# Moving all loads but the first queries to SyncE's queue, with three transfers in place of six for the global values, and the order of the work drawn up anew

## The chip, the cores and the metric

The kernel runs on one core of a Trainium2 chip. The metric is device microseconds of one execution; a profile of one execution comes with it. The engines are named as in the profile: PE is TensorE, DVE is VectorE, ACT is ScalarE, POOL is GpSimd, SP is SyncE. SP does no arithmetic here; it only issues DMA transfers, and so can ACT and POOL. "PEld" is the loading of weights into TensorE, "q1" the queue on which SP issues, "q0" that of POOL, "q10" that of ACT. Lines such as L323 are lines of the kernel before; the diff shifts them by a few in the changed kernel.

## The reference

Attention with a window of 32 positions and 32 global tokens for 8 batches, 8 heads, 512 positions and head size 64; after it an MLP over all 4,352 rows of the result, 512 wide, with 2,048 inner units. In the attention's result and in the MLP all is float32, except that the two weight matrices are float64.

```python
k_all, v_all = concat([k_g, k_l], 2), concat([v_g, v_l], 2)
out_g = softmax(scale * q_g @ k_all.T) @ v_all          # 32 global queries see all 544 keys
s_ll  = where(|i - j| <= 32, scale * q_l @ k_l.T, -1e9) # local queries see a band ...
s_l   = concat([scale * q_l @ k_g.T, s_ll], -1)         # ... and the 32 global keys
out_l = softmax(s_l) @ v_all
x     = concat([out_g, out_l], 2) as (8 * 544, 512)
h     = x @ w_in                                        # 512 -> 2048
out   = (0.5 * h * (1 + erf(h / sqrt(2)))) @ w_out      # 2048 -> 512
```

## The kernel before

**Tiles.** A *unit* is (batch, half, pair): 256 queries of two heads. There are 8 x 2 x 4 = 64 units. Four units give 256 rows of the MLP's input; so the MLP has 16 *pieces* of 256 rows, and a 17th ("g") for the 8 x 32 global queries. A piece goes through the inner units in 16 steps of 128: `h` (L915 to L917, twelve matmuls of 128x256), Gelu, and `mo` (L947 to L949, six matmuls of 128x512 that add into two accumulators). Most products are taken as three: each float32 operand is split into a part rounded to float32r and the rest, and high x high, low x high and high x low are added. The splits are copies (L293 on ACT, L295 on DVE) and subtractions (L303 on POOL or DVE).

**Weights.** `w_load` (L323, L327) brings, for each of the 16 steps, a pair of 512 KB transfers of float64 bits: one of `w_in` (n even) and one of `w_out` (n odd), 32 transfers in all. Steps `w1` to `w5` make float32 of them and split it: L334 and L338 on ACT, L342 on DVE, the rounded copy on DVE or ACT, and the rest on DVE (L303). There are five buffers `wpair`; the sixth pair waits until `w5` of the first is done. After that all weights stay in SBUF. So the first MLP piece can go no faster than the weights are loaded and converted.

**Attention.** For the first 8 units (`NPE`), keys and queries arrive in natural order and are transposed on TensorE (`st_tkn` L516 to L518, `st_tqn` L524). They come in three groups, units 0 and 1, 2 and 3, and 4 to 7; their loads are few and large: `load_kn` (L498, L501), `load_qn` (L508), `load_v` (L443 to L454). The transposes write to PSUM; copies to `kq` (L293 or L295) free that buffer again. For all later units, `load_k` (L409) and `load_q` (L414) bring blocks of 32 columns, four transfers each, which DVE transposes (L480, L481, L529). Then follow the scores (`st_s` L607), the masked minimum (L626 on DVE), the exponential (L471 on ACT), the normalisation, transposes of the weights (`st_t` L678) and the products with the values (L714, L727). The first 8 units (`NF32`) do scores and products in plain float32, all later ones in split form.

**Global values.** For each pair of heads `gu_load` (L831, L833) fills the tile `gvr`, the first 640 columns of `raws`: two transfers bring the 512 local values of each head, and four bring the *same* 32 global values to all four blocks of 32 partitions of the last 128 columns. The matrix they are multiplied with has zeros in three of the blocks, so three of the four copies only keep the operand finite.

**What sets the order.** The order is fixed when the kernel is built, by a planner at its end. Every piece of work is a `step` with an engine (or several to choose from), a duration (`DUR`), needs, buffers that it takes and frees, and a due time. The due time is a formula plus offsets: `OFF`, `OFF0` (one for each kind of step), `UO` (each of the first 16 units), `WO` (each weight transfer) and `XO` (single steps). The planner simulates all engines and the DMA queues and takes, engine by engine, the startable step with the earliest due time; the resulting sequence is written into each engine's program. Engines work through their programs strictly in that order: an instruction that waits holds up all that stands behind it on its engine, and a transfer that waits for a buffer holds up all later transfers of its queue. In the planner's account of the DMA, a queue that has eight transfers in flight takes no further one until the oldest has landed.

Queues in the kernel before: keys, values and global loads on SP (`LKE`, `LVE`, and `nc.sync` written out in `load_k`, `load_q`, `load_g`, `gu_load`); the queries of units 0 to 3 on ACT, those of units 4 to 7 on SP (`LQE`); weight transfers 0 to 15 on POOL (`PQ = 16`), the others on POOL or SP as the planner chooses (`WLE = "ps"`). In effect 21 weight transfers were issued by POOL and 11 by SP.

Of the kernel before, what the change touches and what calls it, by code (L numbers as in the profile page):

```python
# [42 lines left out]
AHEAD = 7.79  # L43
# [7 lines left out]
    "ah": -28.3, "al": 190.6, "c": 36.0, "e": -46.4, "g": -91.8, "gagh": 105.3, "gagl": 84.4, "gah": 95.0,  # L51
    "gal": 279.0, "gex": 364.9, "gh": 34.3, "gl": 79.7, "glv": -266.7, "gmin": 286.5, "gn": -288.8,
    "go": -250.4, "gsh": -53.2, "gsl": -34.5, "gt": -14.4, "gvc": -55.9, "gvl": -83.0, "gx": -45.8,
# [6 lines left out]
}  # L60
OFF0 = {
# [7 lines left out]
PW = 6.14  # L69
PA = 14.0  # L70
UO = [-160.8, -144.7, -220.4, -102.2, -9.8, 29.6, 12.6, -140.0, 234.7, -181.3, -185.0, -209.3, -93.2, -116.0, -6.6, -119.4]
WO = [-219.9, -117.6, -1.3, -67.8, -468.9, -339.8, -131.7, -537.2, 29.9, 77.1, 219.1, 469.3, 117.1, 46.4, -152.0, -101.1, -73.4, 224.9, 158.3, 77.0, 133.5, -203.0, -360.4, 13.9, 12.3, 251.1, 181.3, 156.0, 275.5, 162.0, 44.8, 157.5]
FA = 86.16
PU = 5.1
NF32 = 8
WLE = "ps"
PQ = 16
XO = {
# [17 lines left out]
    ('g', (0, 1), 4): 14.9, ('gagh', (0, 0)): 46.1, ('gagh', (0, 1)): 21.0, ('gagl', (0, 0)): -65.7,  # L96
    ('gagl', (0, 1)): 66.1, ('gah', (0, 0), 0): -6.3, ('gah', (0, 0), 1): 5.8, ('gah', (0, 1), 0): -22.2,
    ('gah', (0, 1), 1): -21.7, ('gal', (0, 0), 0): 15.1, ('gal', (0, 0), 1): 3.3, ('gal', (0, 1), 0): -36.9,
    ('gal', (0, 1), 1): 52.6, ('gex', (0, 0)): 185.8, ('gex', (0, 1)): -30.8, ('gh', (0, 0), 0): -8.2,
# [6 lines left out]
    ('glv', (0, 0), 1): 19.3, ('glv', (0, 1), 0): 49.6, ('glv', (0, 1), 1): -159.6, ('glv', (1, 0), 0): 10.1,  # L106
    ('glv', (1, 0), 1): 0.5, ('gmin', (0, 0)): 135.0, ('gmin', (0, 1)): 4.0, ('gn', (0, 0)): -64.2,
    ('gn', (0, 1)): -43.6, ('go', (0, 0), 0): 117.3, ('go', (0, 0), 1): 87.3, ('go', (0, 1), 0): -62.5,
    ('go', (0, 1), 1): -69.7, ('gsh', (0, 0), 0): 53.1, ('gsh', (0, 0), 1): 24.9, ('gsh', (0, 1), 0): 5.6,
    ('gsh', (0, 1), 1): 16.4, ('gsl', (0, 0), 0): 35.1, ('gsl', (0, 0), 1): 4.3, ('gsl', (0, 1), 0): 40.5,  # L110
    ('gsl', (0, 1), 1): -47.7, ('gt', (0, 0)): 66.4, ('gt', (0, 1)): 17.2, ('gvc', (0, 0), 0): -44.9,
    ('gvc', (0, 0), 1): -265.4, ('gvc', (0, 1), 0): 35.8, ('gvc', (0, 1), 1): -57.0, ('gvl', (0, 0), 0): -51.9,
    ('gvl', (0, 0), 1): -114.2, ('gvl', (0, 1), 0): 51.6, ('gvl', (0, 1), 1): -111.7, ('gvl', (1, 0), 0): -35.8,
    ('gx', (0, 0), 0): 17.2, ('gx', (0, 0), 1): 2.6, ('gx', (0, 1), 0): -23.5, ('gx', (0, 1), 1): -1.5,
    ('gyh', (0, 0), 0): -7.7, ('gyh', (0, 0), 1): 85.4, ('gyh', (0, 1), 0): 167.6, ('gyl', (0, 0), 0): -50.7,
# [1279 lines left out]
```

## Time and profile before

| | |
|---|---|
| median of 3 runs | 1057.9 us (1053.37 to 1058.07) |
| the profiled execution | 1057.46 us, its span 1055.7 us |
| PE busy | 1016.4 us (96%) |
| PEld busy | 903.3 us (86%) |
| ACT busy | 758.4 us (72%) |
| DVE busy | 681.8 us (65%) |
| POOL busy | 352.8 us (33%) |
| mean granted TensorE clock | 0.987 |
| bytes moved by DMA | 71.25 MB, mean 67 GB/s |

Busy shares are means over the whole span. The span has an opening, in which weights and the first units are loaded, a long even stretch, and an end; these are to be read apart, with the view of busy time by stretch. In the lists of waits a row names the waiting instruction, what it waited for, the total in us, the number of waits and the longest. In the chain of waits, each row is a piece of the chain that ended last: start, length, and what it was.

### The profile page before, as it was taken

The page shows a single profiled execution, that of the slowest core. Times are in us where ns is not written, and L with a number is a line of the kernel's source. Part 1 is how long each engine was busy: PE and PEld are TensorE (multiplying, and loading weights), DVE is VectorE, ACT ScalarE, POOL GpSimd, SP SyncE. Part 2 cuts the span into 40 slices and gives each one's busy share as a digit, 9 for nine tenths or more (in the row PEclk, how much of TensorE's full clock was granted, in tenths as well). Part 3 has the DMA queues.
Part 4 walks back from the last instruction along what each step waited for, and adds up shares of the span by engine and source line. Part 5 has one row for each costly group of instructions (what it writes and reads, how often), then busy time and mean ns, then how long its engine had stood idle before and what let it go on. Part 6 is the DMA issues. An engine that isn't in the chain of part 4 may idle for free.

```text
span 1055.7 us, 21420 instructions
## 1 busy us (share of the span) xinstructions
PE 1016.4 (96%) x7100; PEld 903.3 (86%) x7100; DVE 681.8 (65%) x2052; ACT 758.4 (72%) x1628; POOL 352.8 (33%) x410
## 2 busy tenths in 40 slices
PE   5687999999999999999999999999999999999998
PEld 2365898989889898899889898999889898998897
DVE  2887866866775866877677766877677766751000
ACT  3797777977777888677777887787877887763221
POOL 4222233334232532334322523334223423343121
PEclk9698999999999999999999999999999999999999
DMA  9746232223322232223312331323322331110000
GB/s 286 178 149 210 66 80 60 44 64 61 70 38 50 58 83 39 61 45 67 69 33 56 60 85 35 67 40 70 68 36 53 67 78 35 47 26 21 1 21 21
DMA packets 268255, 71.25 MB, mean 67 GB/s; under 512 B 257776, under 2 KB 260336, under 8 KB 268144
## 3 DMA queue, kind: packets, MB, share of 16 engines
q1 hardware_dynamic: 262912, 58.21, 25.4%
q0 software_dynamic: 3024, 11.01, 3.0%
q8 instruction: 56, 0.92, 0.4%
q10 hardware_dynamic: 2208, 0.66, 0.3%
q14 instruction: 55, 0.45, 0.2%
HBM read 60.88 MB, written 8.91 MB: 66 GB/s over the span
## 4 chain that ended last, share of the span: by engine, by line
PE 89%; DMA 4%; DVE 3%; ACT 2%; issue 1%; SPq 1%; ACTq 0%; DVEq 0%
PE h L915 12%; PE h L917 12%; PE h L916 11%; PE acc L947 11%; PE acc L948 11%; PE acc L949 11%; PE o L714 5%; PE s L607 5%; PE t L678 2%; PE go L848 2%; PE sg L758 1%; PE t L679 1%; DMA kn<-in_k_l_dram 1%; DMA wpair<-in_moe_w_out_dram 1%; DMA vr<-in_v_g_dram 1%
## 5 line engine op out<-in xcount | busy, mean ns | idle before, releaser
L915 PE MATMUL h<-xx,w 128*128 128x256 f32 x1088 | 314.5, 289 | 4.0 <-ACT gf L471 4.0
L303 POOL TENSOR_TENSOR gl<-gf,gh 128x512 fp32r<-128x512 f32 x135 | 176.2, 1306 | 400.8 <-ACT gh L293 225.8
L917 PE MATMUL h<-xx,w 128*128 128x256 f32 x1088 | 304.6, 280 | 4.4 <-DVE w L303 4.4
L916 PE MATMUL h<-xx,w 128*128 128x256 f32 x1088 | 304.0, 279 | 0.0
L947 PE MATMUL acc<-w,gh 128*128 128x512 f32 x544 | 221.1, 406 | 0.0
L915 PEld LDWEIGHTS h<-xx,w 128*128 128x128 f32 x1088 | 204.9, 188 | 15.6 <-ACT gf L471 4.6
L948 PE MATMUL acc<-w,gl 128*128 128x512 f32 x544 | 215.1, 395 | 0.0
L949 PE MATMUL acc<-w,gh 128*128 128x512 f32 x544 | 215.0, 395 | 0.0
L916 PEld LDWEIGHTS h<-xx,w 128*128 128x128 f32 x1088 | 205.1, 188 | 6.4
L917 PEld LDWEIGHTS h<-xx,w 128*128 128x128 f32 x1088 | 204.8, 188 | 5.3 <-DVE w L303 5.3
L471 ACT ACT_TABLE_LOAD x141 | 180.9, 1283 | 5.6 <-PE h L917 3.1
L303 POOL TENSOR_TENSOR vs<-vr,vs 128x512 fp32r<-128x512 f32 x56 | 74.6, 1332 | 191.0 <-ACT vs L293 87.3
L471 ACT ACTIVATE gf<-h 128x512 f32<-128x512 f32 x136 | 81.5, 599 | 70.0 <-PE h L917 35.0
L949 PEld LDWEIGHTS acc<-w,gh 128*128 128x128 f32 x544 | 102.5, 188 | 24.5
L471 ACT ACTIVATE a_t<-a_t,sm 128x192 f32<-128x192 f32 x240 | 109.8, 459 | 14.0 <-DVE sm L626 13.2
L947 PEld LDWEIGHTS acc<-w,gh 128*128 128x128 f32 x544 | 102.5, 188 | 14.0 <-issue 0.3
L948 PEld LDWEIGHTS acc<-w,gl 128*128 128x128 f32 x544 | 102.8, 189 | 12.9
L626 DVE CUSTOM_DVE_ANT_0 a_t<-s,mask 128x192 f32<-128x192 f32 x240 | 76.2, 368 | 29.7 <-PE s L607 29.0
L293 ACT ACTIVATE gh<-gf 128x512 fp32r<-128x512 f32 x88 | 55.6, 632 | 49.0 <-PE acc L949 47.8
L698 DVE TENSOR_TENSOR at<-t,at 128x512 fp32r<-128x512 f32 (+1 forms) x112 | 68.1, 616 | 28.9 <-ACT at L293 27.6
L714 PE MATMUL o<-at,vs 128*128 128x256 f32 x448 | 74.2, 288 | 0.3
L293 ACT ACTIVATE at<-t 128x512 fp32r<-128x512 f32 (+1 forms) x112 | 59.1, 541 | 18.6 <-PE t L679 12.0
(138 smaller groups left out, 1573.7 us busy)
## 6 DMA issues: line engine op xcount, KB each, us to landing
raws<-in_v_l_dram SPq DMA_DIRECT2D x64, 128.0 KB, 2.5
out_dram<-ob SPq DMA_DIRECT2D x32, 256.0 KB, 2.3
raws<-in_k_l_dram SPq DMA_DIRECT2D x224, 36.0 KB, 2.0
vr<-in_v_l_dram SPq DMA_DIRECT2D x112, 64.0 KB, 2.1
raws<-in_q_l_dram SPq DMA_DIRECT2D x224, 32.0 KB, 1.9
wpair<-in_moe_w_in_dram POOLq DMA_DIRECT2D x11, 512.0 KB, 8.1
wpair<-in_moe_w_out_dram POOLq DMA_DIRECT2D x10, 512.0 KB, 8.6
wpair<-in_moe_w_out_dram SPq DMA_DIRECT2D x6, 512.0 KB, 5.4
```

Source lines behind the costliest of these rows:

```text
L293: nc.scalar.activation(out=out, in_=in_, func=AF.Copy)
L303: (nc.vector if e == "v" else nc.gpsimd).tensor_sub(**kw)
L471: nc.scalar.activation(func=func, **kw)
L626: nc.vector.tensor_tensor_reduce(out=a_t[:, j, aoff[half][i]:aoff[half][i] + w], in0=s[:, c:c + w], in1=masks[half][:, c:c + w], scale=-SC ...
L698: nc.vector.tensor_sub(out=at[:, 1], in0=st.pop((u, "t", j))[:, :n * P].rearrange("p (n q) -> p n q", q=P), in1=at.bitcast(F32)[:, 0])
L714: nc.tensor.matmul(out=o[:, :, qsl], lhsT=l.rearrange("p s e -> p (s e)"), rhs=r, start=(n == 0), stop=(n == 3), skip_group_check=True)
L915: nc.tensor.matmul(out=h, lhsT=hi, rhs=xh, start=(c == 0), stop=False, skip_group_check=True)
L916: nc.tensor.matmul(out=h, lhsT=hi, rhs=xl, start=False, stop=False, skip_group_check=True)
L917: nc.tensor.matmul(out=h, lhsT=lo, rhs=xh, start=False, stop=(c == NCC - 1), skip_group_check=True)
L947: nc.tensor.matmul(out=acc[t], lhsT=gh[:, f % 2, tsl], rhs=hi, start=(f == a), stop=False)
L948: nc.tensor.matmul(out=acc[t], lhsT=gl[:, f % 2, tsl], rhs=hi, start=False, stop=False)
L949: nc.tensor.matmul(out=acc[t], lhsT=gh[:, f % 2, tsl], rhs=lo, start=False, stop=(f == b - 1))
```

## The change

All weight transfers are issued by SP (`WLE = "s"`, `PQ = 0`), and the queries of units 2 and 3 too; only the two query transfers of units 0 and 1 stay on ACT. `load_k`, `load_q`, `load_g` and `gu_load` take their queue from the planner (`queue(e)`), which is given SP alone for them. `gu_load` issues one transfer of the global values in place of four; the three blocks of partitions that it no longer writes are zeroed once by a memset at the start. The planner's durations of the plain float32 scores are set to 1.2 and 0.65 (1.05 and 0.55 before), its constants and all offsets are new, and so the order of the steps on every engine is another one.

```diff
-    "o": 0.48, "s0": 1.05, "sg0": 0.55, ...
+    "o": 0.48, "s0": 1.2, "sg0": 0.65, ...
...
-AHEAD = 7.79
+AHEAD = 21.61
...
-PW = 6.14
+PW = 7.45
...
-FA = 86.16
-PU = 5.1
+FA = 122.95
+PU = 9.25
...
-WLE = "ps"
-PQ = 16
+WLE = "s"
+PQ = 0
...
-LQE = {0: "a", 2: "a", 4: "s", 6: "s"}
+LQE = {0: "a", 2: "s", 4: "s", 6: "s"}
...
     raws = cp.tile([P, 1184], F32, name="raws")
+    nc.gpsimd.memset(raws[:, 512:640], 0.0)
...
 def load_k(e, u):
-            nc.sync.dma_start(out=kraw[pr], ...)
+            queue(e).dma_start(out=kraw[pr], ...)
...
 def gu_load(e, g, i):
         for j in range(2):
-            nc.sync.dma_start(out=raw[:, j:8:2, :], in_=v_l[b, 2 * p + j].rearrange("(t s) e -> s t e", s=P))
-        for n in range(4):
-            nc.sync.dma_start(out=raw[32 * n:32 * n + 32, 8:10, :], in_=v_g[b, 2 * p:2 * p + 2].rearrange("h s e -> s h e"))
+            queue(e).dma_start(out=raw[:, j:8:2, :], in_=v_l[b, 2 * p + j].rearrange("(t s) e -> s t e", s=P))
+        queue(e).dma_start(out=raw[0:32, 8:10, :], in_=v_g[b, 2 * p:2 * p + 2].rearrange("h s e -> s h e"))
...
-                step(("glv", g, i), gu_load, (g, i), "s", g0 - 12.0 + 2 * i, [], [("gvr", (g, i))], issues=6, size=0.46, ...)
+                step(("glv", g, i), gu_load, (g, i), "s", g0 - 12.0 + 2 * i, [], [("gvr", (g, i))], issues=3, size=0.42, ...)
```

The tables `OFF`, `OFF0`, `UO`, `WO` and `XO` are left out: every number in them is replaced, and `XO` has more entries.

More of the change, by code (lines that the diff above doesn't have):

```diff
@@ L50 @@
 OFF = {
-    "ah": -28.3, "al": 190.6, "c": 36.0, "e": -46.4, "g": -91.8, "gagh": 105.3, "gagl": 84.4, "gah": 95.0,
-    "gal": 279.0, "gex": 364.9, "gh": 34.3, "gl": 79.7, "glv": -266.7, "gmin": 286.5, "gn": -288.8,
-    "go": -250.4, "gsh": -53.2, "gsl": -34.5, "gt": -14.4, "gvc": -55.9, "gvl": -83.0, "gx": -45.8,
[6 rows of a table removed]
+    "ah": -211.1, "al": 160.1, "c": -16.3, "e": 13.1, "g": -47.0, "gagh": 62.8, "gagl": 136.9,
+    "gah": 55.5, "gal": 309.1, "gex": 12.5, "gh": -21.6, "gl": 127.7, "glv": -432.6, "gmin": 325.2,
+    "gn": -164.9, "go": -134.3, "gsh": 61.6, "gsl": -288.7, "gt": 23.5, "gvc": -30.4, "gvl": 21.8,
[6 rows of a table added]
 }
 OFF0 = {
[4 rows of a table removed]
[4 rows of a table added]
 }
@@ L68 @@
 FH = 8
-PW = 6.14
+PW = 7.45
 PA = 14.0
-UO = [-160.8, -144.7, -220.4, -102.2, -9.8, 29.6, 12.6, -140.0, 234.7, -181.3, -185.0, -209.3, -93.2, -116.0, -6.6, -119.4]
-WO = [-219.9, -117.6, -1.3, -67.8, -468.9, -339.8, -131.7, -537.2, 29.9, 77.1, 219.1, 469.3, 117.1, 46.4, -152.0, -101.1, -73.4, 224.9, 158.3, 77.0, 133.5, -203.0, -360.4, 13.9, 12.3, 251.1, 181.3, 156.0, 275.5, 162.0, 44.8, 157.5]
-FA = 86.16
-PU = 5.1
+UO = [-392.3, -324.5, -466.6, -352.7, -219.4, -4.3, 79.2, -212.3, 297.9, -231.0, -224.0, -213.8, -190.2, -142.1, -206.7, -54.7]
@@ L75 @@
+WO = [-233.6, -272.1, 18.8, 79.4, -468.3, -440.1, 10.1, -401.7, 160.7, 127.2, 284.8, 552.5, 98.0, 88.9, -36.8, -133.1, -19.5, 157.0, 203.3, 10.3, 3.9, -137.0, -448.4, 17.1, -86.0, 50.4, 66.1, -73.3, 84.2, -14.7, -33.4, 3.9]
+FA = 122.95
+PU = 9.25
 NF32 = 8
-WLE = "ps"
-PQ = 16
+WLE = "s"
+PQ = 0
 XO = {
[17 rows of a table removed]
[L96 to L99, printed above, removed]
[6 rows of a table removed]
[L106 to L115, printed above, removed]
[54 rows of a table removed]
-    ('sga', (0, 0, 2)): 14.5, ('sga', (0, 0, 3)): -31.2, ('sga', (0, 1, 0)): 74.4, ('sga', (0, 1, 1)): 6.0,
-    ('sga', (0, 1, 2)): 18.2, ('sga', (0, 1, 3)): 3.3, ('sga', (1, 0, 0)): -162.1, ('sga', (1, 0, 1)): -106.7,
-    ('sga', (1, 0, 2)): -11.1, ('sgc', (1, 0, 0)): -7.9, ('sgc', (1, 0, 1)): 68.0, ('sgc', (1, 0, 2)): -81.1,
[42 rows of a table removed]
[19 rows of a table added]
+    ('gagl', (0, 0)): -47.6, ('gagl', (0, 1)): 17.8, ('gah', (0, 0), 0): 36.0, ('gah', (0, 0), 1): 34.5,
+    ('gah', (0, 1), 0): -22.0, ('gah', (0, 1), 1): 38.1, ('gal', (0, 0), 0): -245.5, ('gal', (0, 0), 1): 91.2,
+    ('gal', (0, 1), 0): 137.9, ('gal', (0, 1), 1): 13.8, ('gex', (0, 0)): 53.2, ('gex', (0, 1)): -193.4,
[7 rows of a table added]
+    ('glv', (0, 1), 0): 62.5, ('glv', (0, 1), 1): -201.2, ('glv', (1, 0), 0): -62.3, ('glv', (1, 0), 1): -12.2,
+    ('gmin', (0, 0)): 276.7, ('gmin', (0, 1)): -18.9, ('gn', (0, 0)): -31.4, ('gn', (0, 1)): 12.5,
+    ('go', (0, 0), 0): 1.7, ('go', (0, 0), 1): 229.8, ('go', (0, 1), 0): -314.7, ('go', (0, 1), 1): -76.3,
+    ('gsh', (0, 0), 0): -60.2, ('gsh', (0, 0), 1): -125.5, ('gsh', (0, 1), 0): -74.6, ('gsh', (0, 1), 1): 15.3,
+    ('gsl', (0, 0), 0): 39.4, ('gsl', (0, 0), 1): 83.0, ('gsl', (0, 1), 0): 28.1, ('gsl', (0, 1), 1): -71.6,
+    ('gt', (0, 0)): 79.7, ('gt', (0, 1)): -124.9, ('gvc', (0, 0), 0): -116.3, ('gvc', (0, 0), 1): -243.4,
+    ('gvc', (0, 1), 0): -55.5, ('gvc', (0, 1), 1): 56.6, ('gvc', (1, 0), 0): 66.2, ('gvl', (0, 0), 0): -40.7,
+    ('gvl', (0, 0), 1): -73.6, ('gvl', (0, 1), 0): -2.3, ('gvl', (0, 1), 1): -173.1, ('gvl', (1, 0), 0): 139.3,
+    ('gx', (0, 0), 0): -103.3, ('gx', (0, 0), 1): 81.1, ('gx', (0, 1), 0): -105.6, ('gx', (0, 1), 1): 50.1,
+    ('gyh', (0, 0), 0): -41.4, ('gyh', (0, 0), 1): 27.2, ('gyh', (0, 1), 0): 248.2, ('gyh', (0, 1), 1): -30.0,
+    ('gyl', (0, 0), 0): -233.3, ('gyl', (0, 0), 1): 138.1, ('gyl', (0, 1), 0): 36.2, ('gyl', (0, 1), 1): 43.6,
[57 rows of a table added]
+    ('sga', (0, 0, 1)): -68.9, ('sga', (0, 0, 2)): 214.8, ('sga', (0, 0, 3)): -2.0, ('sga', (0, 1, 0)): 202.1,
+    ('sga', (0, 1, 1)): 67.5, ('sga', (0, 1, 2)): 18.5, ('sga', (0, 1, 3)): 35.9, ('sga', (1, 0, 0)): -165.4,
+    ('sga', (1, 0, 1)): 112.4, ('sga', (1, 0, 2)): -156.5, ('sga', (1, 0, 3)): 44.0, ('sgc', (1, 0, 0)): 55.3,
+    ('sgc', (1, 0, 1)): 141.6, ('sgc', (1, 0, 2)): -79.3, ('sgc', (1, 0, 3)): 49.7, ('t', (0, 0, 0), 0): -299.1,
[42 rows of a table added]
@@ L408, in load_k @@
         for j, pr, es in quads():
-            nc.sync.dma_start(out=kraw[pr], in_=k_l[b, 2 * p + j].rearrange("(c r) e -> r c e", r=32)[:, k0:k0 + 9, es])
+            queue(e).dma_start(out=kraw[pr], in_=k_l[b, 2 * p + j].rearrange("(c r) e -> r c e", r=32)[:, k0:k0 + 9, es])
     def load_q(e, u):
@@ L413, in load_q @@
         for j, pr, es in quads():
-            nc.sync.dma_start(out=qraw[pr], in_=q_l[b, 2 * p + j].rearrange("(c r) e -> r c e", r=32)[:, 8 * half:8 * half + 8, es])
+            queue(e).dma_start(out=qraw[pr], in_=q_l[b, 2 * p + j].rearrange("(c r) e -> r c e", r=32)[:, 8 * half:8 * half + 8, es])
     gq = raws[0:SG, 0:2 * NP * D]
@@ L428, in load_g @@
             for j, pr, es in quads():
-                nc.sync.dma_start(out=dst[pr], in_=src[b].rearrange("(p j) r e -> j r p e", j=2)[j][:, :, es])
+                queue(e).dma_start(out=dst[pr], in_=src[b].rearrange("(p j) r e -> j r p e", j=2)[j][:, :, es])
     def load_v(e, u, n=1):
@@ L1141, in attn_mlp @@
                 step(("gal", g, i), gu_al, (g, i), "v", g0 + 3.0 + 2 * i, [("gah", g, i)], [], [("s", (g, "t"))])
-                step(("glv", g, i), gu_load, (g, i), "s", g0 - 12.0 + 2 * i, [], [("gvr", (g, i))], issues=6, size=0.46, after=("glv", *pi) if pi[0] else None)
+                step(("glv", g, i), gu_load, (g, i), "s", g0 - 12.0 + 2 * i, [], [("gvr", (g, i))], issues=3, size=0.42, after=("glv", *pi) if pi[0] else None)
                 step(("gvc", g, i), gu_vc, (g, i), "va", g0 + 1.0 + 2 * i, [("glv", g, i), ("late",)], [("vgs", (g, i))])
```

266 rows, old and new, of tables (DUR, OFF, OFF0, XO) are left out of this document.

## The prediction

> **What bounds the kernel now.** The time of the profiled execution is 1057.46 us, its span 1055.7 us; the 1.8 us around the span are carried along unchanged. The median of the three runs is 1057.9 us, so a sum against the profiled execution stands 0.4 us under the median. I first cut the span into three stretches with the view of busy time by stretch (columns: stretch, its length, busy time and count of PE, PEld, DVE, ACT, POOL, then granted clock, DMA share, GB/s).
>
> ```profile
> span 1055.7 us, 21420 instructions
> ...
> 0.00:140.00 140.00, 106.64 (x696) 81.84 (x697) 97.89 (x229) 103.00 (x206) 45.37 (x79) 0.90 0.60 172
> 140.00:1045.00 905.00, 903.85 (x6381) 817.01 (x6381) 583.26 (x1822) 652.98 (x1420) 307.45 (x331) 1.00 0.25 52
> 1045.00:1055.70 10.70, 5.91 (x27) 4.47 (x25) 0.69 (x1) 2.43 (x4) 0.00 (x0) 0.99 0.18 49
> ```
>
> From 140 to 1045 us TensorE is idle for 905.00 - 903.85 = 1.15 us at full clock. No new order can gain anything worth naming there; it could only lose. The last 10.7 us are the end of the last MLP and its stores, which keep their form. What can move lies in the first 140 us, where TensorE is idle for 140 - 106.64 = 33.4 us. The same view in steps of 10 us shows where:
>
> ```profile
> 0.00:10.00 10.00, 4.47 (x18) 2.81 (x20) 0.75 (x1) 3.22 (x7) 9.28 (x29) 1.00 0.88 215
> 10.00:20.00 10.00, 3.23 (x12) 1.28 (x9) 1.27 (x8) 3.96 (x11) 2.99 (x11) 1.00 1.06 359
> ...
> 30.00:40.00 10.00, 3.58 (x15) 2.12 (x15) 9.76 (x14) 9.33 (x13) 2.04 (x4) 0.57 0.84 210
> 40.00:50.00 10.00, 9.00 (x44) 5.23 (x43) 7.00 (x24) 6.67 (x21) 2.35 (x4) 0.57 0.60 120
> ...
> 90.00:100.00 10.00, 6.73 (x47) 5.39 (x45) 4.03 (x8) 5.47 (x6) 0.02 (x1) 0.99 0.93 306
> 100.00:110.00 10.00, 5.40 (x18) 4.63 (x19) 9.93 (x16) 9.20 (x16) 2.91 (x2) 0.50 0.66 217
> ```
>
> Three holes: at 10 to 20 us (6.8 us idle), at 30 to 40 us (6.4 us idle), at 90 to 110 us (3.3 + 4.6 = 7.9 us idle). The second and third are followed by a granted clock of 0.57 and 0.50, and that costs again: 0.43 x (3.58 + 9.00) = 5.4 us and 0.50 x 5.40 = 2.7 us of what counts as busy. So the holes weigh 6.8, 11.8 and 10.6 us, together 29.2 us. The first 10 us (5.5 us idle) are mostly the time until the first loads land. Next I asked for TensorE's waits in these stretches (total, times, longest), and for the pieces of the chain of waits there (start, length, what):
>
> ```profile
> PE kp L516 <- DMA kn<-in_k_l_dram: 4.4, 1, 4.4
> PE kp L518 <- DMA kn<-in_k_l_dram: 2.4, 1, 2.4
> ...
> PE kp L516 <- ACT kq L293: 8.2, 1, 8.2
> ...
> PE h L917 <- DVE w L303: 4.4, 2, 4.2
> ```
>
> ```profile
> 6.49 12.15 DMA kn<-in_k_l_dram
> ...
> 30.99 1.01 ACT wpair L334
> 32.00 2.06 ACT wpair L338 x2
> 34.06 1.04 ACT wpair L334
> 35.11 1.00 ACT wpair L338
> ...
> 85.92 11.77 DMA wpair<-in_moe_w_out_dram
> 97.70 2.16 DMA raws<-in_k_l_dram
> ```
>
> The first hole is a key load of 12.15 us. The second is ScalarE: 1.01 + 2.06 + 1.04 + 1.00 = 5.1 us of weight conversion stand in its order ahead of the copy that frees the PSUM buffer of the next key transpose. The third is a weight load of 11.77 us, with a key load behind it.
>
> **The change, part by part.**
>
> (a) All 32 weight loads move to SP's queue. These rows are the weights' issues (min/median/max ns), SP's wait for a weight buffer in the first 130 us, and a stretch in which SP was kept from issuing:
>
> ```profile
> L323 POOL DMA_DIRECT2D wpair<-in_moe_w_in_dram x11: 748/751/915, 3.9 to 86.3; - x11
> L327 POOL DMA_DIRECT2D wpair<-in_moe_w_out_dram x10: 547/547/637, 4.8 to 87.0; - x10
> L327 SPq DMA_DIRECT2D wpair<-in_moe_w_out_dram x6: 423/504/505, 72.5 to 105.8; - x6
> L323 SPq DMA_DIRECT2D wpair<-in_moe_w_in_dram x5: 372/385/404, 72.1 to 105.4; - x5
> ```
>
> ```profile
> SPq L323 <- DVE w L303: 13.0, 2, 8.2
> ```
>
> ```profile
> 14.74 8.91 SPq L498 DMA_DIRECT2D kn<-in_k_l_dram  x2
> ```
>
> In the last row two key loads hold SP for 8.91 us before they are issued: a full queue stops SP too. POOL loses 11 x 0.751 + 10 x 0.547 = 13.7 us of issuing. It is busy for 45.4 of the first 140 us, so I cost that at nothing: its idle time hides it. SP gains 11 x 0.385 + 10 x 0.504 = 9.3 us, spread over some 100 us. Uncovered, each issue would delay the load behind it by about 0.5 us.
>
> What matters is the order of the bytes. Landing times (issue to landing, median, us), first in the first 20 us, then from 84 to 99 us:
>
> ```profile
> qn<-in_q_l_dram ACTq DMA_DIRECT2D x4, 128.0 KB, 4.0
> ```
>
> ```profile
> wpair<-in_moe_w_out_dram SPq DMA_DIRECT2D x3, 512.0 KB, 11.8
> wpair<-in_moe_w_in_dram SPq DMA_DIRECT2D x2, 512.0 KB, 7.4
> wpair<-in_moe_w_in_dram POOLq DMA_DIRECT2D x2, 512.0 KB, 9.2
> wpair<-in_moe_w_out_dram POOLq DMA_DIRECT2D x1, 512.0 KB, 11.4
> raws<-in_q_l_dram SPq DMA_DIRECT2D x4, 32.0 KB, 11.7
> ```
>
> Before, GpSimd starts weights from 3.9 us on, while SP's key loads are still being issued; the DMA engines are full and the second group of keys takes 12.15 us. On one queue that group can go ahead of the weights. Then it lands like the first queries, which were issued ahead of most weights, in 4.0 us, that is up to 8.1 us earlier, of which TensorE's waits return at most 4.4 + 2.4 = 6.8 us. If the new order puts weights in front, nothing is won. Between 0 and 6.8 I take **4 us**: nearer to the upper end, since the first loads have a queue to themselves as soon as GpSimd issues none. Late next are then ScalarE's and VectorE's conversions of weights that arrive a little later.
>
> (b) The order of ScalarE, VectorE and TensorE is drawn up anew. For the second hole the price lies between 0 (the copy stands behind conversions again) and 11.8 us (hole and slow clock gone). I take **4 us**, a third, since the same conversions have to fit in somewhere else. For the third hole it lies between 0 and 10.6 us: eight weight transfers were issued in a burst (the 3, 2, 2 and 1 above), and both a share of the burst and the small loads behind it can be set otherwise. But buffers come free no sooner than VectorE converts. I take **3 us**.
>
> (c) The new wait: all 16 pairs, and not a third of them, now stand in SP's in-order queue. The first five find free buffers, eleven wait for one; of the waits seen, two took 13.0 us. Behind a waiting weight load stand all key, query and value loads, and behind those VectorE's transposes and TensorE. Bounds: 0 (SP waits when nothing is due) and 10.6 us (one more hole such as the third). I take **-2 us**, nearest to the fact that SP's longest wait, 8.2 us, is already there.
>
> The Trainium skill ("DMA: Bandwidth & Descriptors", "Queues, rings and completion order") says that a DMA engine takes turns between the queues that have work for it, packet by packet. By that, a small load on a queue of its own keeps its turn beside a stream of weights, and loses it when both share one queue; that speaks against this change. The rows agree only in part: the keys had a queue apart from the weights and still took 12.15 us. By the rule alone, term (a) would be a loss, unless the keys are issued first.
>
> (d) The second queries (two transfers) leave ACT's queue, and the global values take one transfer in place of four, made safe by one memset. Rows: the four query issues on ACT, four global-value issues on SP, a memset of similar size.
>
> ```profile
> 0.76 2.21 ACTq L508 DMA_DIRECT2D qn<-in_q_l_dram  x4
> ...
> 27.37 1.91 SPq L833 DMA_DIRECT2D raws<-in_v_g_dram  x4
> ...
> 36.05 0.31 POOL L459 MEMSET vre<- 64x256 f32 x1
> ```
>
> ACT is rid of 2.21 / 2 = 1.1 us at a time when it waits for TensorE anyway; SP issues these queries instead, behind the keys they are used with, so nothing. Three issues of 1.91 / 4 = 0.48 us are saved in each of 32 loads, 46 us of SP over the whole kernel, nearly all of it in the stretch where TensorE has no idle time: nothing. The memset adds 0.3 us on POOL before its first real work at 26 us: nothing; uncovered, 0.3 us.
>
> Sum: 4 + 4 + 3 - 2 = **9 us less, 1057.5 - 9 = 1048.5 us**.
>
> **The rivals.**
>
> *No change.* The holes move but do not shrink. For it: the stage ends with the last weight conversion, and VectorE is nearly full through it:
>
> ```profile
> 20.00:90.00 70.00, 57.22 (x405) 41.29 (x405) 60.27 (x152) 58.58 (x125) 20.36 (x29) 0.88 0.62 169
> ```
>
> 60.27 of 70 us is 86%. Four us won ahead of 20 us are then lost again while the conversions are worked off. Against it: VectorE does only 0.75 + 1.27 = 2.0 us of work in the first 20 us and pauses for 6 us at 90 to 100 us. Its time: 1057, between 1053 and 1062.
>
> *Slower: SP's queue holds back small loads.* One weight load waits for its buffer on SP, eight transfers follow, and keys and queries behind them land 11.7 us late, as at 84 to 99 us, but twice. Each such hole costs 10.6 us with the slow clock after it: 1057.5 + 10.6 = **1068**. It decides once a second wait of about 8 us falls where TensorE has no attention work in store. For it: five of 16 pairs on SP made one such hole. Against it: three of the eight transfers of that burst were GpSimd's and would now be queued after SP's own. The skill's rule on turns between queues belongs to this rival: sharing one queue makes it likelier.
>
> *Much faster: all three holes close.* 1057.5 - 29.2 = **1028**. For it: they have three causes, all of them order. Against it: each part of the first 100 us is short of VectorE and ScalarE time.
>
> *The change doesn't do what it says*, that is, the loads run in the same sequence as before whichever queue carries them: then it is the no-change case.
>
> **How the numbers follow.** Forecast 0.48 (own range 1040 to 1052), no change 0.20, slower 0.20, all holes closed 0.12. For this kernel 0.5% (5.3 us) is about what can be told from no change. Faster by more than that: 0.48 + 0.12 = 0.60; within: 0.20; slower: 0.20. The range has to leave out no more than 2 in 10: it drops half of the fastest case and something over half of the slower one, so 1032 to 1064.
>
> **What would show it.** (a) The second key group lands well before 15 us, and TensorE's two waits for keys are gone. (b) The granted clock stays at 1.00 from 30 to 50 us, and idle time of TensorE in the first 140 us falls from 33 to about 25 us. (c) SP's waits for weight buffers stay around 13 us. From 140 to 1045 us nothing changes. The forecast is wrong if that stretch shows more than 3 us of idle time, or if a hole of 8 us or more stands between 50 and 130 us with keys or queries named as its releaser.

## The result and the profile after

| | before | after |
|---|---|---|
| median of 4 runs each, us | 1057.12 (1053.37 to 1058.07) | 1045.34 (1043.78 to 1045.48) |
| ratio, 95% interval | | 0.9892 [0.9865, 0.9918] |
| span of the profiled execution, us | 1055.7 | 1043.6 |
| mean granted TensorE clock | 0.987 | 0.985 |

The changed kernel is faster by 11.8 us on the medians and by 12.1 us on the spans; 9 us were forecast. In the changed kernel the lines stand 7 or 8 further down: the subtraction of step `w5` is L310 (L303 before), the copies are L300 and L302 (L293 and L295), the key transposes L524 (L516), the third product of `h` is L924 (L917).

Busy time by stretch, after (the columns are those of the same view before: stretch, length, PE, PEld, DVE, ACT, POOL, granted clock, DMA share, GB/s):

```profile
span 1043.6 us, 21145 instructions
...
10.00:20.00 10.00, 9.78 (x48) 5.30 (x47) 7.93 (x28) 6.97 (x22) 0.83 (x1) 1.00 0.78 215
20.00:30.00 10.00, 7.86 (x34) 4.30 (x33) 7.30 (x31) 7.67 (x24) 2.06 (x5) 0.78 0.93 272
30.00:40.00 10.00, 3.63 (x22) 2.46 (x23) 8.53 (x17) 9.05 (x15) 0.29 (x2) 0.50 0.87 207
40.00:50.00 10.00, 9.03 (x56) 6.54 (x58) 6.95 (x19) 6.10 (x16) 0.97 (x2) 0.70 0.69 179
...
60.00:70.00 10.00, 5.28 (x32) 4.88 (x33) 4.90 (x16) 9.17 (x18) 1.25 (x3) 0.50 1.06 353
...
90.00:100.00 10.00, 10.00 (x67) 9.08 (x66) 7.64 (x8) 8.68 (x11) 2.26 (x1) 1.00 1.04 308
100.00:110.00 10.00, 9.34 (x62) 7.86 (x61) 6.97 (x7) 9.01 (x13) 3.55 (x2) 1.00 0.25 88
...
0.00:140.00 140.00, 115.32 (x766) 92.00 (x767) 100.09 (x248) 108.31 (x215) 39.65 (x62) 0.89 0.64 175
140.00:1030.00 890.00, 890.00 (x6292) 804.08 (x6291) 567.18 (x1798) 638.42 (x1395) 309.59 (x335) 1.00 0.24 50
```

TensorE's idle time in the first 140 us falls from 33.4 to 24.7 us. The first hole is gone (idle at 10 to 20 us: 6.8 before, 0.2 now), and so is the third (90 to 110 us: 7.9 before, 0.7 now). The second stands as it was (30 to 40 us: 6.4 idle both times), and one of 4.7 us has come at 60 to 70 us, where 1.0 us was idle before. The slow clock has not been won back: at 20 to 50 us and at 60 to 70 us it costs 0.22 x 7.86 + 0.50 x 3.63 + 0.30 x 9.03 + 0.50 x 5.28 = 8.9 us, against 5.4 + 2.7 = 8.1 us before. Cut finer, in steps of 2 us, the view shows that after's clock is at 0.50 from 26 us on, so the slow stretch begins ahead of the second hole and not behind it. Behind 140 us nothing is idle until the end of the MLP.

TensorE's waits, after: the first row from the first 20 us, the second from 20 to 40 us, the third from 60 to 80 us.

```profile
PE kp L524 <- DMA kn<-in_k_l_dram: 5.0, 2, 3.7
...
PE kp L524 <- DVE kq L302: 4.6, 1, 4.6
...
PE o L735 <- ACT ao L300: 4.8, 1, 4.8
```

The key waits that are left lie in the first 10 us. The second hole has changed its releaser: ScalarE's copy of `kq` was late before, now it is VectorE's, which stands behind two conversions. The new hole is of the same kind, on ScalarE (timeline of ScalarE, after):

```profile
60.83 1.10 ACT L341 ACTIVATE wpair<-wpair 128x1024 int32<-128x1024 uint16 x1 [3.70 <-DMA wpair<-in_moe_w_out_dram]
61.84 0.44 ACT L479 ACTIVATE ae<-ae,sm 128x192 f32<-128x192 f32 x1
```

A conversion waits 3.70 us for its weights, and the exponentials that TensorE needs stand behind it in the same program.

The issues of SP at the start (start, length), and the landing times of loads issued in the first 20 us, after:

```profile
5.79 0.61 SPq L509 DMA_DIRECT2D kn<-in_k_l_dram  x1
...
8.20 0.90 SPq L330 DMA_DIRECT2D wpair<-in_moe_w_in_dram  x1
```

```profile
kn<-in_k_l_dram SPq DMA_DIRECT2D x1, 256.0 KB, 3.1
...
kn<-in_k_l_dram SPq DMA_DIRECT2D x3, 64.0 KB, 2.9
```

The planner does put the first two groups of keys ahead of the first weight. The load of 12.15 us before is one of 64 KB; after, the three of that size take 2.9 us (median). The 256 KB load belongs to the third group of keys. SP's waits in the first 130 us, after:

```profile
SPq L422 <- DVE qt L537: 12.9, 2, 10.7
SPq L330 <- DVE w L310: 8.2, 2, 7.7
```

The waits for weight buffers are 8.2 us, not more than the 13.0 us before, though all weights now wait there.

Last, the conversions of the weights. These rows are all subtractions of step `w5` (min/median/max ns, first and last start in us), before and after:

```profile
L303 DVE TENSOR_TENSOR w<-wpair,w x16: 1180/1224/1228, 32.8 to 125.8; 128x1024 fp32r<-128x1024 f32 x16
```

```profile
L310 DVE TENSOR_TENSOR w<-wpair,w x14: 1216/1225/2076, 23.7 to 108.4; 128x1024 fp32r<-128x1024 f32 x14
L310 POOL TENSOR_TENSOR w<-wpair,w x2: 2394/2420/2446, 57.3 to 112.1; 128x1024 fp32r<-128x1024 f32 x2
```

The last weight pair is ready at 125.8 + 1.2 = 127.0 us before and at 112.1 + 2.4 = 114.5 us after: 12.5 us sooner, where the span falls by 12.1 us. The conversions begin 32.8 - 23.7 = 9.1 us sooner, and their whole train is 94.2 - 90.8 = 3.4 us shorter.

### The profile page after: what moved, and what is told of

It is laid out like the page before. It is cut to its first block, busy times and chain, and to the rows that moved or that the text cites. A ratio compares the mean times of both kernels' runs of the same rounds, so it can differ in the third digit from the quotient of the medians.

```text
span 1043.6 us, 21145 instructions
## 1 busy us (share of the span) xinstructions
PE 1014.7 (97%) x7100; PEld 903.6 (87%) x7100; DVE 668.0 (64%) x2046; ACT 749.2 (72%) x1613; POOL 349.6 (33%) x397
## 4 chain that ended last, share of the span: by engine, by line
PE 90%; SPq 3%; DMA 3%; DVE 2%; ACT 1%; issue 1%; DVEq 0%; ACTq 0%
PE h L922 12%; PE acc L954 12%; PE acc L956 12%; PE h L924 12%; PE acc L955 12%; PE h L923 12%; PE o L722 5%; PE s L615 5%; PE t L686 3%; DMA wpair<-in_moe_w_out_dram 2%; PE go L855 2%; PE sg L766 1%; PE t L687 1%; DMA raws<-in_q_l_dram 1%; SPq L459 1%
## 5 line engine op out<-in xcount | busy, mean ns | idle before, releaser
L310 POOL TENSOR_TENSOR gl<-gf,gh 128x512 fp32r<-128x512 f32 x135 | 178.0, 1318 | 410.3 <-ACT gh L300 267.7
L924 PE MATMUL h<-xx,w 128*128 128x256 f32 x1088 | 304.3, 280 | 0.9 <-DVE w L310 0.9
L924 PEld LDWEIGHTS h<-xx,w 128*128 128x128 f32 x1088 | 204.7, 188 | 1.3 <-DVE w L310 1.3
L300 ACT ACTIVATE gh<-gf 128x512 fp32r<-128x512 f32 x108 | 68.2, 632 | 97.2 <-PE acc L956 96.8
L310 POOL TENSOR_TENSOR vs<-vr,vs 128x512 fp32r<-128x512 f32 x56 | 74.5, 1329 | 154.9 <-DVE vs L302 47.5
L954 PEld LDWEIGHTS acc<-w,gh 128*128 128x128 f32 x544 | 102.1, 188 | 14.3 <-issue 0.3
L300 ACT ACTIVATE at<-t 128x512 fp32r<-128x512 f32 (+1 forms) x112 | 58.9, 539 | 22.8 <-PE t L689 16.2
```

The source lines that it names most:

```text
L300: nc.scalar.activation(out=out, in_=in_, func=AF.Copy)
L310: (nc.vector if e == "v" else nc.gpsimd).tensor_sub(**kw)
L924: nc.tensor.matmul(out=h, lhsT=lo, rhs=xh, start=False, stop=(c == NCC - 1), skip_group_check=True)
L954: nc.tensor.matmul(out=acc[t], lhsT=gh[:, f % 2, tsl], rhs=hi, start=(f == a), stop=False)
```

## The experiments

Ratios are to the kernel before on the same chip, whose medians were 1055.3 us (first four kernels), 1055.52 us (the next four) and 1056.45 us (the last four). In the edits, `move(x, y)` takes step x out of the finished order and puts it in front of step y of the same engine (behind it with `True`); each engine's program follows that order.

**1. All weights on GpSimd's queue, the order of after.**

```diff
 # w_load, both transfers
-            queue(e).dma_start(
+            nc.gpsimd.dma_start(
```

> The changed kernel with its order of work kept as it is, step by step, but all 32 weight transfers issued by GpSimd in place of SyncE. Theory: what the change won comes from the sequence in which bytes and engine work are put, and this kernel keeps it nearly (the first weights can start some 2 us earlier, the later ones wait behind GpSimd's own work). So 1045 to 1049 us, the first hole of TensorE (10 to 20 us) stays under 2 us. Rival: the queue itself matters (slower issue, packets of two queues taking turns); then 1052 us or more and weights land later than the 6.3 us of the changed kernel.

Measured: 1045.87 us, ratio 0.9919 [0.9896, 0.9941], span 1042.7 us: 0.5 us above the median of after, 2.9 us by the ratios, with intervals that overlap. The queue that carries the weights is not what gained the 12 us, and SP's waits for weight buffers, absent here, cost after nothing that can be seen. The landing time of the 256 KB key load (row 1), SP's waits for small-load buffers (row 2, first 130 us) and a wait of TensorE (row 3, from 20 to 40 us) do differ:

```profile
kn<-in_k_l_dram SPq DMA_DIRECT2D x1, 256.0 KB, 10.5
...
SPq L422 <- DVE qt L537: 36.2, 3, 17.1
...
PE kp L524 <- DMA kn<-in_k_l_dram: 3.9, 2, 3.6
```

With weights on the other queue from 6.77 us on, that load takes 10.5 us beside them. In after it takes 3.1 us: SP issues it at about 19 us, when the three weights ahead of it have landed (issued by 9.8 us, 6.3 us each), and the fourth is issued at 22.4 us. This agrees with the rule on turns between queues that the prediction took from the Trainium skill ("DMA: Bandwidth & Descriptors", "Queues, rings and completion order"), with another consequence than I drew: here a load that goes ahead of the weights on the shared queue has the engines to itself, and on a queue of its own it has a share. TensorE waits 3.6 us for these keys here and not at all in after, and still the two times cannot be told apart.

**2. The order of before, all weights on SP.** The second keys now stand ahead of the weights by their place in the old order; nothing else of the change is made.

```diff
 # kernel before, w_load, both transfers
-            queue(e).dma_start(
+            nc.sync.dma_start(
```

> The kernel before with its order of work kept, but all 32 weight transfers issued by SyncE, each at its old place in the sequence; that puts the second group of keys ahead of the first weights. Theory: the 12.15 us key load falls to about 4 us, the first hole of 6.8 us shrinks to under 2 us, and most of that reaches the end: 1051 to 1053 us. Rival (no carry): the hole at 10 to 20 us goes but the conversion of weights ends at the same time, 1056 to 1058 us. Second rival (SyncE's queue holds back small loads): 1060 us or more with a new hole after 50 us.

Measured: 1049.74 us, ratio 0.9948 [0.9926, 0.9971], span 1047.2 us. So one queue, with the load sequence that follows from it and no new order of the engines, brings 5.6 us on the medians (8.5 us on the spans), a little more than expected. As 1 shows the queue itself to be worth nothing that can be seen, the gain is put down to the sequence. Stretches of this kernel, then a wait of TensorE, then its `w5` steps:

```profile
10.00:20.00 10.00, 10.00 (x38) 5.09 (x36) 6.00 (x25) 6.88 (x19) 0.83 (x1) 1.00 1.07 300
20.00:30.00 10.00, 2.91 (x13) 1.37 (x11) 9.68 (x22) 9.21 (x18) 1.22 (x4) 0.75 1.04 345
...
90.00:100.00 10.00, 6.45 (x33) 5.68 (x33) 9.49 (x18) 8.06 (x11) 1.49 (x2) 0.84 0.85 252
100.00:110.00 10.00, 9.71 (x61) 8.53 (x59) 7.42 (x12) 8.32 (x16) 2.37 (x2) 0.99 0.47 135
```

```profile
PE kp L516 <- ACT kq L293: 7.6, 2, 7.1
```

```profile
L303 DVE TENSOR_TENSOR w<-wpair,w x16: 1186/1226/1228, 25.8 to 118.1; 128x1024 fp32r<-128x1024 f32 x16
```

The first hole is closed; a hole of 7.1 us stands right behind it at 20 to 30 us, because the same copy on ScalarE is late again. Of the third hole 3.55 + 0.29 = 3.8 us are left of 7.9, and one of 3.6 us has come at 50 to 60 us. But the conversions begin 7.0 us sooner and end at 118.1 + 1.2 = 119.3 us, 7.7 us sooner.

**3. After, with the first ten weights ahead of the second keys.**

```diff
+    for n in range(10):
+        move(("wl", n), ("lk", (0, 0, 2)))
```

> The changed kernel with the first ten weight transfers moved ahead of the second group of keys on SyncE's queue, all other engines in the same order. Theory: the keys land some 14 us later (ten transfers of 512 KB at about 1.4 us), the hole at 10 to 20 us returns with 7 us or more, and most of it reaches the end: 1051 to 1058 us. Rival (no carry): weights arrive earlier in exchange and the end moves by under 2 us, 1044 to 1047 us.

Measured: 1053.05 us, ratio 0.9987 [0.9969, 1.0004], span 1049.9 us: 7.7 us above the median of after, and 10 us by the ratios, which is nearly all of the gain; the interval holds 1, so against before no gain is shown. A stretch, TensorE's longest wait, and the last `w5` steps of this kernel:

```profile
10.00:20.00 10.00, 0.56 (x4) 0.00 (x0) 1.27 (x8) 0.00 (x0) 0.00 (x0) 1.00 1.07 383
```

```profile
PE qgp L584 <- DMA raws<-in_q_g_dram: 13.6, 1, 13.6
```

```profile
L310 POOL TENSOR_TENSOR w<-wpair,w x2: 2409/2428/2447, 67.9 to 118.1; 128x1024 fp32r<-128x1024 f32 x2
```

On one queue the small loads wait out the weights ahead of them: 13.6 us at one stroke. The hole is 9.4 us deep in this stretch, and the last pair is ready at 120.5 us, 6.0 us later than in after.

**4. After, with the four transfers of the global values again.**

```diff
-        queue(e).dma_start(out=raw[0:32, 8:10, :], ...)
+        for n in range(4):
+            queue(e).dma_start(out=raw[32 * n:32 * n + 32, 8:10, :], ...)
```

> The changed kernel with the global values loaded four times again, so six transfers a pair; order kept. Theory: SyncE has time in the long even stretch and TensorE is full there, so 1045 us, within 1 us. Rival: SyncE's queue is a bound in the changed kernel; then 96 issues of 0.48 us show as 2 us or more.

Measured: 1046.03 us, ratio 0.9919 [0.9899, 0.9939], span 1046.1 us. The ratio of after, 0.9892, lies just below this interval, but the two intervals overlap. The median is 0.7 us above that of after; by the ratios it would be 2.9 us. So no effect is shown, and a loss of 2 us, as the rival has it, is not ruled out.

**5. Each hole closed by one move, and both.** 5a moves VectorE's copy of `kq` in front of a conversion, for the hole at 30 to 40 us; 5b moves the conversion that waits for its weights behind the exponentials, for the hole at 60 to 70 us.

```diff
+    move(("q1", (0, 1, 2)), ("w3", 4))                 # 5a
+    move(("w1", 10), ("ah", (0, 1, 0), 1), True)       # 5b
```

> The changed kernel with one step moved: VectorE's copy of unit (0, 1, 2)'s queries stands ahead of two weight conversions and a normalisation, not behind them. In the changed kernel TensorE waits 4.6 us for it (at 32.5 to 37.1 us, clock 0.50). Theory (TensorE's holes carry to the end): the wait falls under 1 us and the time by 2 to 5 us, to 1040 to 1043 us. Rival (the stage ends with the last weight conversion on ACT and VectorE, holes ahead of it cost nothing): 1044 to 1046 us although the wait is gone.

> The changed kernel with another single step moved: ScalarE's first conversion of the sixth weight pair, which waits 3.7 us for its load, stands behind the exponentials and the copy that TensorE needs at 59 to 64 us, not ahead of them. Theory: TensorE's wait of 4.8 us falls under 1 us, the slow clock after it goes too (0.50 at 60 to 70 us), 1040 to 1043 us. Rival (no carry): 1044 to 1046 us.

> Both moves together. Theory: the two gains add up, 1036 to 1041 us. Rival (no carry): 1044 to 1046 us; and if one gain hides the other, 1040 to 1043 us.

Measured: 5a 1044.50 us, ratio 0.9896 [0.9868, 0.9924]; 5b 1042.39 us (1042.01 to 1042.86), 0.9876 [0.9843, 0.9909]; both 1044.71 us, 0.9896 [0.9869, 0.9924]. 5a takes the wait of 4.6 us away and idle at 30 to 40 us falls from 6.4 to 3.3 us, yet no gain can be told from none; the clock in that stretch stays at 0.50. 5b is the fastest kernel measured: 3.0 us below the median of after, and its runs do not overlap those of after; by the ratios it is 1.7 us, and there the intervals overlap. Its rows, a stretch and the last `w5` steps:

```profile
60.00:70.00 10.00, 8.59 (x63) 7.79 (x64) 8.08 (x20) 9.94 (x13) 1.72 (x4) 0.66 1.07 356
```

```profile
L310 POOL TENSOR_TENSOR w<-wpair,w x2: 2405/2425/2445, 57.7 to 108.5; 128x1024 fp32r<-128x1024 f32 x2
```

The new hole is down from 4.7 to 1.4 us, and the last pair is ready at 110.9 us, 3.6 us sooner. So 5a and both come out in the range of the rival (no carry), 5b in that of the theory. The two gains do not add; with both moves a wait of TensorE for weights comes in behind the start of the MLP (waits of TensorE in the first 140 us, both moves):

```profile
PE h L924 <- DVE w L310: 2.3, 2, 1.6
```

**6. Dummy matmuls in both holes of after, to keep the clock up.** Their results are not used; the 24 in each hole stand as 48 rows in the trace.

```diff
+    def warm(n):
+        t = ps_o.tile([P, 512], F32, name="warm", tag="acc1")
+        for _ in range(n):
+            nc.tensor.matmul(out=t[0:64, 0:P], lhsT=ident[:, 0:64], rhs=ident, start=True, stop=True)
...
 # st_tkn of unit (0, 1, 3) and st_o0 of unit (0, 1, 0)
+            warm(24)
```

> The changed kernel with 24 additional small matmuls, whose results nobody reads, in TensorE's order at each of the two holes (ahead of the keys of unit (0, 1, 3) and ahead of the product of unit (0, 1, 0)). They fill time in which TensorE waits anyway and keep it active. Theory (idle time lowers the granted clock, and the slow clock costs some 4 to 5 us in the changed kernel at 30 to 50 and 60 to 70 us): the clock there rises to 0.8 or more and the time falls by 2 to 4 us. Rival: the clock does not follow, or TensorE's speed there doesn't set the end: within 1 us of 1045 us.

By the figures above the slow clock in these stretches costs 0.50 x 3.63 + 0.30 x 9.03 + 0.50 x 5.28 = 7.2 us rather than 4 to 5. Measured: 1044.14 us, ratio 0.9892 [0.9864, 0.9921], mean clock 0.997. Stretches of this kernel, then pieces of TensorE's timeline (start, length):

```profile
30.00:40.00 10.00, 8.17 (x53) 7.31 (x53) 8.71 (x22) 9.84 (x19) 0.29 (x2) 0.83 0.86 217
40.00:50.00 10.00, 8.58 (x78) 6.26 (x76) 7.05 (x20) 5.01 (x11) 0.97 (x2) 1.00 0.76 186
...
60.00:70.00 10.00, 8.89 (x86) 8.46 (x86) 6.14 (x19) 8.55 (x17) 3.29 (x4) 1.00 1.06 339
```

```profile
33.37 7.12 PE L521 MATMUL warm<-ident 128*64 128x128 f32 x48
40.42 0.44 PE L531 MATMUL kp<-ident,kn 128*128 128x128 f32 x2
...
61.05 5.34 PE L521 MATMUL warm<-ident 128*64 128x128 f32 x47
```

The clock rose (0.50, 0.70 and 0.50 became 0.83, 1.00 and 1.00), and the time did not fall by anything that can be seen. In the first hole the rise is not the dummies' alone: from 30 to 32 us, before the first of them, the clock is already 1.00 here and 0.50 in after. And this is no clean test of the clock's worth: 7.12 + 5.34 = 12.5 us of dummies are longer than the two waits they fill (4.6 and 4.8 us). The next key transpose starts at 40.42 us; in after it started at 37.06 us:

```profile
37.06 0.69 PE L524 MATMUL kp<-ident,kn 128*128 128x128 f32 x2 [4.57 <-DVE kq L302]
```

Of these 3.4 us, 1.2 us were there before the dummies (the query transpose ahead of them starts at 33.00 us, in after at 31.80 us). So the dummies first delayed the work by some 2 us, and the faster clock may just have paid for that. What full clock alone is worth stays open.

**7. After, with the last conversion step done twice.** If the end of the conversions sets the time, its 2.42 us come on top; if it only marks it, nothing does.

```diff
-        sub(e, out=w[:, :, 512:1024], in0=wraw.pop(n)[:, :, :, 1].bitcast(F32), ...)
+        x = wraw.pop(n)[:, :, :, 1].bitcast(F32)
+        for _ in range(2 if n == 30 else 1):
+            sub(e, out=w[:, :, 512:1024], in0=x, ...)
```

> The changed kernel with the very last step of weight conversion (GpSimd's subtraction for the sixteenth pair, 2.42 us, ending at 114.5 us in the changed kernel) done twice; nothing else is moved. In the ten profiles so far the span minus the end of the last conversion is 928 to 930 us. Theory A: the end of the last conversion itself decides when TensorE can go on; then 1047 to 1048 us (2.4 us more). Theory B: TensorE has been full for some 40 us by then and the conversions only keep pace with it; the end of the last one is a mark and not a cause; then 1045 to 1046 us, and the difference rises from 929 to about 927 us.

Measured: 1047.47 us (1046.09 to 1049.18), ratio 0.9912 [0.9887, 0.9937]; after on the same chip 1045.11 us (1044.25 to 1047.20), 0.9892 [0.9868, 0.9916]. The medians differ by 2.4 us, as the first theory has it, but the runs and intervals overlap. The doubled step on GpSimd, and TensorE's longest wait from 110 to 120 us, in this kernel:

```profile
110.18 4.92 POOL L310 TENSOR_TENSOR w<-wpair,w 128x1024 fp32r<-128x1024 f32 x2
```

```profile
PE h L926 <- POOL w L310: 1.5, 1, 1.5
```

In after on the same chip the list of TensorE's waits is empty for that stretch. So the last step has less than 2.4 us to spare: 1.5 us of the extra work came out as idle time at that spot. The span less the end of the last conversion is 929.2 us in this profile, where the second theory expected about 927. Both speak for a cause; the total time leaves it unsettled.

**8. More moves on top.** 8a is 5b with four weight loads issued ahead of the value loads; 8b is 5a with these loads and with the conversions of the fifth and sixth pair moved in their programs (`w1` to `w3` of weight 8, `w1` of weight 10; that last move stands in place of the one of 5b).

```diff
+    for n, ref in ((8, (0, 1, 0)), (9, (0, 1, 0)), (10, (1, 0, 0)), (11, (1, 0, 0))):   # 8a and 8b
+        move(("wl", n), ("lv", ref))
+    move(("w1", 10), ("w2", 8), True)                  # 8b only
+    move(("w1", 8), ("ah", (0, 0, 1), 1), True)
+    move(("w2", 8), ("q1", (0, 1, 3)), True)
+    move(("w3", 8), ("k1", (0, 1, 3)))
```

> The second single move again (ScalarE's exponentials ahead of the conversion that waits), and besides the fifth and sixth pair of weights are issued by SyncE ahead of value loads that are due later (at about 36 to 42 us in place of 41 to 55 us). Theory: the opening of the new order is short of converted weights because loads stand late in SyncE's queue; then ScalarE's waits for weights (1.6 and 3.7 us in the changed kernel) go and the time falls by 1 to 3 us under the 1042.4 us of that move alone. Rival (ScalarE's and VectorE's work itself is the bound): 1042 to 1043 us.

> Both single moves, the fifth and sixth pair of weights issued earlier, and the conversions of these pairs moved into gaps of ScalarE and VectorE at 42 to 50 us. Theory: with conversions ahead of the MLP's need, TensorE's holes before the start of the MLP can be closed for gain: 1037 to 1041 us, first matmul of the MLP's second product at 72 us or before (77.0 us in the changed kernel) and under 3 us of idle time between it and 140 us. Rival (the two moves got in each other's way for another reason): 1042 to 1045 us.

Measured: 1044.99 us, ratio 0.9888 [0.9862, 0.9913], and 1043.98 us, 0.9880 [0.9859, 0.9901]. Neither beats 5b, and both miss what their theory forecast. In 8a ScalarE's waits for weights in the first 80 us fall from 9.5 to 4.9 us, but a wait of 3.7 us for a value load, now behind the weights, appears. In 8b the first `mo` matmul starts at 72.7 us and TensorE is idle for 2.6 us from there to 140 us, nearly as its theory asked, and the time is that of its rival.

**9. After once more, beside 7, 8a and 8b**, for the comparisons above.

> The changed kernel once more, to have it beside the other kernels on the same chip: 1044 to 1046 us.

Measured: 1045.11 us, span 1045.4 us.

**All profiles in one table.** "Last pair ready" is the last start of the `w5` rows plus their median duration, as worked out above.

| kernel | span, us | last pair ready, us | span less that, us |
|---|---|---|---|
| before | 1055.7 | 127.0 | 928.7 |
| 2 | 1047.2 | 119.3 | 927.9 |
| after | 1043.6 | 114.5 | 929.1 |
| 9 (after again) | 1045.4 | 115.2 | 930.2 |
| 1 | 1042.7 | 113.7 | 929.0 |
| 3 | 1049.9 | 120.5 | 929.4 |
| 4 | 1046.1 | 117.2 | 928.9 |
| 5a | 1042.6 | 112.5 | 930.1 |
| 5b | 1040.2 | 110.9 | 929.3 |
| 5, both | 1042.3 | 112.3 | 930.0 |
| 6 | 1043.5 | 114.2 | 929.3 |
| 7 | 1044.3 | 115.1 | 929.2 |
| 8a | 1043.1 | 113.7 | 929.4 |
| 8b | 1041.9 | 112.5 | 929.4 |

Spans differ by 15.5 us, the last column by 2.3 us, and by 1.1 us between the two profiles of after itself. Whatever was changed, and whichever hole it closed, the span is close to the moment at which the last weights are ready plus 929 us. The start of the first `mo` does not go with it: 74.4 us before, 77.0 us after. Nor does the account of holes fit as closely: the span less TensorE's idle time and slow clock in the first 140 us (in steps of 10 us) lies between 1010.0 and 1015.0 us in the 13 profiles without dummies.

This is a relation over 14 profiles and not yet a cause. TensorE hardly ever waits for weights in the stretch in which the last pairs are converted (waits from 60 to 140 us, after and 5b; before, it was 4.4 us):

```profile
PE h L924 <- DVE w L310: 0.9, 2, 0.7
```

```profile
PE h L924 <- DVE w L310: 0.2, 1, 0.2
```

So the conversions keep just ahead of TensorE's need. Whether their end sets the time, or both follow from the same order of work, only 7 asks, and it leaves that open.

## Why the prediction was right

**The forecast, 9 us less.** Measured 11.8. The mechanism was the forecast one in outline: loads in another sequence and a new order close holes of TensorE in the first 140 us and leave the rest alone. Of its terms, (a) was too small, (c) too dark, and (b) put together from the wrong parts.

**(a) Keys ahead of weights: 4 us.** Right in mechanism and too small in size. The sequence (2) brings 5.6 us on the medians, and putting weights first (3) costs 7.7 us. The first hole closes almost wholly. The step that failed is "late next are then ScalarE's and VectorE's conversions of weights that arrive a little later": the conversions did not come later. ScalarE's first two conversion steps start at 13.3 and 14.3 us in both kernels, so their weights came no later. The third stands behind exponentials whose scores need those keys (ScalarE's waits for them in the first 130 us, before and 2):

```profile
ACT a_t L471 <- DVE sm L626: 9.6, 2, 8.1
```

```profile
ACT a_t L471 <- DVE sm L626: 2.5, 2, 1.5
```

With that wait gone it starts at 18.3 us in place of 25.4 us, and the `w5` steps begin 7.0 us sooner. So the hole's 6.8 us were not eaten up by the stage's end, which came sooner too.

**(b) The new order: 4 for the second hole, 3 for the third.** Its sum is near, its parts are not, and that is luck. The second hole stayed whole (6.4 us idle, clock 0.50), which was its lower bound of 0, and closing half of it (5a) gained nothing that could be told from none. The third hole went almost wholly: 7.9 - 0.7 = 7.2 us of idle time and the 2.7 us of slow clock behind it. But the new hole gives back 4.7 - 1.0 = 3.7 us and 0.50 x 5.28 = 2.6 us; net 3.6 us. By the time, the step from 2 to after, which holds (b) and (c), is worth 4.4 us on the medians and (0.9948 - 0.9892) x 1057 = 5.9 us by the ratios; 4 + 3 - 2 = 5 were forecast for it. That share is what is left over when the sequence is taken off; no run shows which steps of the new order earn it. What the order did that I had not priced: it moved rounding copies and two subtractions of the conversions off VectorE. All work on the weight tiles `wpair`, first 130 us, before and after (POOL before is the issuing of loads):

```profile
sum 130.00, DVE 46.70 ACT 42.93 POOL 13.95; mean DVE 15.57 ACT 14.31 POOL 4.65
```

```profile
sum 130.00, DVE 40.57 ACT 48.87 POOL 4.84; mean DVE 13.52 ACT 16.29 POOL 1.61
```

VectorE has 6.1 us less of it. That this makes the shorter train of conversions (90.8 us against 93.5 us in 2) is argued, not shown; it was not tried alone.

**(c) New waits on SP: -2 us.** Not there. The waits fell from 13.0 to 8.2 us, and taking all weights off SP (1) changed the median by 0.5 us, with intervals that overlap. As a place where a loss can arise the step was right: with weights ahead of small loads (3), one wait of 13.6 us stands where SP's queue holds them back. The order of the loads, not the queue, decides.

**(d) Queries and global values: 0.** No effect of the global values is shown (4), within the 2 to 3 us that the run could have missed. The second queries and the memset were not undone alone.

**The rivals.** "No change" had the premise right, that the stage ends with the last weight conversion, and the conclusion wrong: it took that end as fixed, and it came 12.5 us sooner. (That the stage ends there fits every profile; as a cause it is not shown.) "Slower" is real as a mechanism, but the planner's order avoids it. Run 3 forces a relative of it, with weights ahead of small loads and no wait for a buffer, and costs 7.7 us, not 10.6. "All holes close" did not come: of its three holes the second still stands, and a new one is there at 60 to 70 us. The loads did run in another sequence.

**What would show it.** (a) and (c) came out as said, except that SP's waits fell below 13 us. (b) did not: the clock at 30 to 50 us was 0.50 and 0.70, not 1.00, while idle time fell to 24.7 us as said (25). Neither sign of a wrong forecast appeared. From 140 us on, 1.2 us of idle time vanished as well. The weight of holes was too coarse a measure: I added idle time and slow clock hole by hole, and by that account 5a should have gained 3.6 us (3.1 us of idle time and 0.5 us of slow clock in the first 140 us); it gained 0.8 us. The measure that fits the profiles more closely is when the last weight pair is ready.

## What to carry to other kernels

Where a stage loads, converts and uses something at once, look first for the event at which the stage ends (here, by the fit of 14 profiles, the last converted weight pair) and ask of each edit whether it comes sooner; closing a hole of the busiest engine may gain less than the hole's own length, as 5a did (3.1 us of idle time at 30 to 40 us, 0.8 us of time). When small loads and a bulk stream share the DMA engines, put the small ones first in the same queue, and then check each in-order engine program for a bulk step that waits for its data with urgent work behind it (5b gained 1.7 us by the ratios and 3.0 us on the medians with one such move, by the ratios not clear of the noise). Two such moves need not add, so time them one by one.

## What the runs showed of the hardware

One DMA queue carried as much as two: at 60 to 70 us 353 GB/s moved in after, with all loads on SP, and 359 GB/s in 1, with the weights on GpSimd:

```profile
60.00:70.00 10.00, 7.08 (x42) 5.59 (x41) 8.46 (x29) 10.00 (x19) 5.30 (x6) 0.66 1.02 359
```

And the granted clock stood higher where TensorE was kept busy: with 24 small float32 matmuls in the hole at 60 to 70 us (47 of their rows take 5.34 us) it was 1.00 in that stretch, against 0.50 in after, with no gain in time that can be seen. From 58 to 60 us, ahead of these matmuls, it was 1.00 and 0.94, so the two kernels came to the hole nearly alike.
